# Strassen's seven block products for the first products of five pairs of F chunks in an exact-float32 MLP beside linear attention

## The chip, the cores and the metric

One of the cores of a Trainium2 chip runs the whole kernel. The metric is device time in microseconds (us), the median of several runs. The engines are called PE (TensorE, the matrix multiplier), DVE (VectorE), ACT (ScalarE), POOL (GpSimd) and SP (SyncE, which issues nearly all DMAs).

## The reference

A parallel block: one layernorm feeds linear attention with a learned feature map and an MLP, and both results are added to the input. B = 1, S = 2048 tokens, D = 640, H = 32 heads of 20, F = 1728; all arrays are float32.

```python
x  = A_x
xn = layernorm(x)
# attention
q, k, v = (xn @ wqkv) split into 3 x H heads of 20
pq, pk  = per head q @ w_phi, k @ w_phi
phi     = concat(softmax(p), softmax(-p))            # 40 features a head
o       = phi_q (phi_k^T v) / (phi_q (phi_k^T 1) + 1e-6)
A       = o @ wo
# MLP (its own layernorm: the block norms xn again)
y       = layernorm(xn)
B       = gelu(y @ w1 + b1) @ w2 + b2
return x + A + B
```

## The kernel before

**Arithmetic.** float32 is kept by splitting every operand into a high and a low part of the matmul type (`split`, L57-67: ACT copies to the high part, L61; another engine subtracts to get the low part, L64). A product is then three matmuls into one PSUM bank, `mm3` (L69-72): high·high (L70), high·low (L71), low·high (L72).

**Stages.** The tokens are four blocks of 512 (b0 to b3), D is five chunks of 128 (`KC`), F fourteen chunks of 128 (the last has 64). Activations lie transposed, features on partitions and tokens on columns.

1. First MLP pass (about 0 to 210 us): blocks b0 and b1. Beside it the generator `prep` makes what the next stage needs, one step per product: the folded q and k weights, and the normed tokens y of blocks b2 and b3 (L569-590: POOL subtracts the mean, DVE scales, ACT makes the high part, DVE the low part, two DMAs store both).
2. Projections and feature maps (about 210 to 441 us, `features`, matmuls at L673). For each token tile the features are transposed and stored to DRAM (`store_phi`).
3. Second MLP pass (441 to about 640 us): blocks b2 and b3, with attention's second half beside it.
4. Output projection (from about 640 us, L1119-1136), with sums into the accumulators and the stores.

**An MLP pass.** It works in groups g = 0 to 6 of two F chunks (a pair). `passes` (L267-309) does one group for one token block: for both chunks `first` (L256) makes z = w1·y as five `mm3` into one of banks 0 to 2; `gelu` (L263) applies the bias and gelu on ACT (L264) from the bank and splits the hidden block into high and low parts (ACT L61, DVE L64). The generator yields there; then for each of the five output chunks m two `mm3` (one for each F chunk) go into one of banks 5 to 7 and DVE adds the bank to the accumulator in SBUF (L309). The loop at L1081 starts the first products of the next group or block before it finishes the second products of the one before, so each gelu has the other block's second products to hide behind. Weights arrive by `fetch` (two DMAs of 320 KB, raw tiles r1 and r2) and are split by `take` (L229-254: ACT makes the high part, POOL the low part) a group ahead, into one of four slots w0 to w3 for each F chunk, w1 and w2 together.

**Attention beside the second pass.** `attend` (L1060) is a generator that `mm3`'s callers step once after each product (`next(self.beside, None)`). For each token block it loads 11 groups of features (tiles e); ACT makes the high part (L960), POOL the low part (L961), PE does two matmuls against kvs (L967, L968), ACT moves half of the result (L977), DVE adds (L978) into the output tile `ob`. `quotients` then moves denominators through DRAM, spreads their reciprocals with shuffles on DVE (L1011) and multiplies on POOL (L1013). Output tiles of b0 and b1 lie in a pool of their own (oB), those of b2 and b3 take over acc0 and acc1, which are free by then. `split` (L1017) divides them for the projection.

**What sets the order.** PE's order is written out by hand throughout. In the first pass and from pair 1 of the second pass on, DVE, ACT and POOL keep the written order too (`manual_schedule`); between them a scheduler orders these engines. SP's queue is ordered by a scheduler. Each engine works its list in order, and a tile that is taken again makes its new writer wait for its last reader.

The driver of the second pass, before:

```python
            this = mlp.passes(g, b, ws)
            next(this)
            for _ in before:
                pass
            before = this
...
            if g < 6:
                wn.append(mlp.take(2 * g + b))
                if 2 * g + b < 13:
                    mlp.fetch(2 * g + 1 + b)
```

Of the kernel before, what the change touches and what calls it, by code (L numbers as in the profile page):

```python
# [15 lines left out]
P = 128  # L16
# [35 lines left out]
def tile_kernel(ctx: ExitStack, tc: tile.TileContext, x, xT, wkT, wqT, wv, wphi, wo, w1, b1, w2, b2,  # L52
# [24 lines left out]
    ones1 = cp.tile([1, P], F32, name="ones1")  # L77
# [13 lines left out]
    r_dram = {n: tc.dram_tile([n, 8, P], F32, name=f"r{n}") for n in (1, 2)}  # L91
    a_dram = [tc.dram_tile([P, KC, 512], F32, name=f"a{b}") for b in range(2)]
# [108 lines left out]
    def load_rows(b):  # L201

        mr = mtile(5)
# [7 lines left out]
    class Mlp:  # L211
# [55 lines left out]
        def passes(self, g, b, ws, hid=None):  # L267
# [27 lines left out]
            for m in range(KC):  # L295
# [12 lines left out]
                else:  # L308
                    nc.vector.tensor_tensor(acc[b][:, m, :], pw, acc[b][:, m, :], op=ALU.add)  # L309

# [230 lines left out]
    def prep():  # L541
# [13 lines left out]
        mr = load_rows(2)  # L555
# [6 lines left out]


        def load(b, c):
            xc = fp.tile([P, D], F32, name="raw")[:, :512]
            nc.sync.dma_start(xc, xT[c * P:(c + 1) * P, b * 512:(b + 1) * 512])
            return xc

        for b in range(2, 4):  # L569
            ahead = load(b, 0)  # L570
            if b == 3:
                mr = load_rows(3)
            for _ in range(5 if b == 2 else 10):
                yield
            for c in range(KC):
                xc, ahead = ahead, load(b, c + 1) if c < KC - 1 else None
                nc.gpsimd.tensor_tensor(xc, xc, mr[:, 0], op=ALU.subtract)
                for _ in range(3):
                    yield
                nc.vector.tensor_tensor(xc, xc, mr[:, 1], op=ALU.mult)  # L580
                for _ in range(2):
                    yield
                hl = fp.tile([P, 2, KC, G5], F32R, name="t").rearrange("p a c f -> p a (c f)")[:, :, :512]
                nc.scalar.activation(hl[:, 0], xc, AF.Copy)
                for _ in range(2):
                    yield
                nc.vector.tensor_tensor(hl[:, 1], xc, f(hl[:, 0]), op=ALU.subtract)
                for p in range(2):
                    nc.sync.dma_start(y_dram[b - 2][p][:, c, :], f(hl[:, p]))
                yield  # L590
# [193 lines left out]
    for t, i in [(t, i) for t in range(14) for i in range(4)] + TAIL:  # L784
# [35 lines left out]
        if (t, i) == (11, 0):  # L820
            mlp = Mlp((0, 3, 2, 1), ((1, 2), (0, 3)))
            mlp.ph = ptile
            mlp.fetch(0)
        if (t, i) == (12, 3):
            with tc.issue_after(evac):
                ws = [mlp.take(0)]
            mlp.fetch(1)
        if (t, i) == (15, 3):
            w, late = mlp.take_parts(1)
            ws.append(w)  # L830
# [3 lines left out]
    mlp.fetch(2)  # L834
    wkv.close()

# [6 lines left out]
    kvs = bp.tile([P, 11, P], F32R, name="kvs")  # L843
    fs = ExitStack()
# [20 lines left out]
    load_acc(3)  # L865

# [50 lines left out]
    class Attention:  # L917

        def __init__(self, b, bank):
            self.b, self.n, self.bank = b, 0, bank  # L920
            self.ob = op.tile([P, KC, 512], F32, name=f"ob{b}") if b < 2 else acc01.tile([P, KC, 512], F32, name=f"acc{b - 2}")
# [61 lines left out]
        def quotients(self):  # L983
# [25 lines left out]
            for c in range(KC + 1):  # L1009
                if c < KC:  # L1010
                    nc.vector.stream_shuffle(rx[:, c, :], rx[:, c, :], SPREAD)  # L1011
                if c:
                    nc.gpsimd.tensor_tensor(ob[:, c - 1, :], ob[:, c - 1, :], rx[:, c - 1, :], op=ALU.mult)  # L1013
                for i in range(3):
                    yield

        def split(self, c, eng):  # L1017
# [15 lines left out]
            if c == KC and b < 2:  # L1033

                acc[b] = op.tile([P, KC, 512], F32, name=f"ob{b}")
                nc.sync.dma_start(acc[b], a_dram[b])

    def load_wo():

        for p, wd in enumerate(wo_dram):  # L1040
            w = wp.tile([P, 4, D], F32R, name=f"w{(2, 1)[p]}")
# [16 lines left out]
    ep = op = rx = None  # L1058
# [22 lines left out]
    for g in range(7):  # L1081
        for b in range(2, 4):
            if b == 2:
                wn = []
            if (g, b) == (0, 2):
                with tc.issue_after(subs["q", 15].ins):
                    wn.append(mlp.take(2))
                mlp.fetch(3)
# [111 lines left out]
```

## Time and profile before

| | |
|---|---|
| time, median of 3 runs | 720.99 us (720.93 to 721.01) |
| profiled execution, span | 719.3 us |
| profiled execution, time around the span (median less span) | 1.7 us |
| DMA traffic | 91.88 MB, mean 128 GB/s |
| HBM read, written | 63.51 MB, 27.73 MB |
| POOL, 441 to 470 us | 14.93 us busy |

The span runs from the first to the last instruction of one profiled execution. Rows of a time line give start, duration, engine, line and operation, output and inputs; rows of groups give the count, the busy time, the mean of one in ns, and the idle time of the engine just before them with what ended it. A matmul's row has the time from its start to its modelled end, and these overlap.

### The profile page before, as it was taken

The page shows a single profiled execution, that of the slowest core. Times are in us where ns is not written, and L with a number is a line of the kernel's source. Part 1 is how long each engine was busy: PE and PEld are TensorE (multiplying, and loading weights), DVE is VectorE, ACT ScalarE, POOL GpSimd, SP SyncE. Part 2 cuts the span into 40 slices and gives each one's busy share as a digit, 9 for nine tenths or more (in the row PEclk, how much of TensorE's full clock was granted, in tenths as well). Part 3 has the DMA queues.
Part 4 walks back from the last instruction along what each step waited for, and adds up shares of the span by engine and source line. Part 5 has one row for each costly group of instructions (what it writes and reads, how often), then busy time and mean ns, then how long its engine had stood idle before and what let it go on. Part 6 is the DMA issues. An engine that isn't in the chain of part 4 may idle for free.

```text
span 719.3 us, 9640 instructions
## 1 busy us (share of the span) xinstructions
PE 710.7 (99%) x3411; PEld 598.2 (83%) x3411; DVE 477.6 (66%) x787; ACT 323.0 (45%) x530; POOL 384.1 (53%) x332
## 2 busy tenths in 40 slices
PE   8989999999999999999999999999999999999998
PEld 7868888888888888888888887888888888888887
DVE  7776754757554788788898887635565566766432
ACT  6434454334334544545435446346565556530200
POOL 3521223345045997897878879346577787403000
PEclk9999999999999999999999999999999999999999
DMA  9803642656411227326302506943443443164122
GB/s 328 264 8 109 195 133 84 179 158 192 139 74 73 92 82 232 85 97 214 80 0 55 130 3 204 229 144 111 135 128 127 134 153 94 49 230 132 74 87 74
DMA packets 60454, 91.88 MB, mean 128 GB/s; under 512 B 7014, under 2 KB 31366, under 8 KB 59038
## 3 DMA queue, kind: packets, MB, share of 16 engines
q1 hardware_dynamic: 60102, 91.25, 40.7%
q8 instruction: 27, 0.44, 0.2%
q14 instruction: 21, 0.17, 0.1%
q10 hardware_dynamic: 304, 0.01, 0.0%
HBM read 63.51 MB, written 27.73 MB: 127 GB/s over the span
## 4 chain that ended last, share of the span: by engine, by line
PE 87%; DVE 3%; POOL 3%; ACT 1%; issue 1%; DMA 0%; SPq 0%; POOLq 0%
PE bank L673 23%; PE bank L70 18%; PE bank L72 18%; PE bank L71 18%; PE bank L743 2%; PE bank L499 2%; POOL m L708 2%; PE bank L967 1%; PE bank L968 1%; POOL m L719 1%; PE bank L305 1%; PE bank L285 1%; PE bank L304 1%; PE bank L286 1%; DVE sm L711 1%
## 5 line engine op out<-in xcount | busy, mean ns | idle before, releaser
L673 PE MATMUL bank<-wkh,y 128*128 128x512 f32 (+1 forms) x480 | 139.5, 364 | 0.0
L64 POOL TENSOR_TENSOR w<-r,w 128x640 fp32r<-128x640 f32 x52 | 83.3, 1619 | 95.6 <-ACT w L61 64.7
L70 PE MATMUL bank<-y,w 128*128 128x512 f32 (+1 forms) x334 | 129.8, 389 | 1.0 <-ACT m L264 1.0
L71 PE MATMUL bank<-y,w 128*128 128x512 f32 (+1 forms) x334 | 129.2, 387 | 0.0
L72 PE MATMUL bank<-y,w 128*128 128x512 f32 (+1 forms) x334 | 129.2, 387 | 0.0
L70 PE MATMUL bank<-m,w 128*128 128x512 f32 x260 | 102.4, 394 | 2.6 <-DVE acc L309 2.3
L72 PE MATMUL bank<-m,w 128*128 128x512 f32 x260 | 101.3, 389 | 0.0
L71 PE MATMUL bank<-m,w 128*128 128x512 f32 x260 | 101.2, 389 | 0.0
L673 PEld LDWEIGHTS bank<-wkh,y 128*128 128x128 f32 x480 | 87.5, 188 | 13.3
L309 DVE TENSOR_TENSOR acc<-bank,acc 128x512 f32<-128x512 f32 x120 | 81.1, 684 | 19.8 <-PE bank L72 11.8
L673 PE MATMUL bank<-wkl,y 128*128 128x512 f32 (+1 forms) x240 | 87.4, 364 | 0.0
L64 DVE TENSOR_TENSOR m<-m,m 128x512 fp32r<-128x512 f32 (+1 forms) x54 | 43.7, 814 | 65.5 <-ACT m L61 65.3
L70 PEld LDWEIGHTS bank<-y,w 128*128 128x128 f32 x334 | 62.7, 188 | 13.9 <-ACT m L264 1.2
L72 PEld LDWEIGHTS bank<-y,w 128*128 128x128 f32 x334 | 62.7, 188 | 12.8
L71 PEld LDWEIGHTS bank<-y,w 128*128 128x128 f32 x334 | 62.7, 188 | 12.5
L264 ACT ACTIVATE m<-bank,b1t 128x512 f32<-128x512 f32 (+1 forms) x54 | 36.2, 671 | 65.2 <-PE bank L72 61.0
L709 ACT ACTIVATE m<-m,rs_all 128x1280 f32<-128x1280 f32 x32 | 43.7, 1365 | 42.9 <-POOL m L708 42.9
L70 PEld LDWEIGHTS bank<-m,w 128*128 128x128 f32 x260 | 48.8, 188 | 14.4 <-DVE acc L309 3.5
L961 POOL TENSOR_TENSOR e<-e,m 128x512 fp32r<-128x512 f32 x28 | 36.2, 1295 | 41.8 <-ACT m L960 35.8
L711 DVE TENSOR_REDUCE sm<-m 128x64 f32<-128x1280 f32 x32 | 47.4, 1481 | 15.5 <-ACT m L709 15.4
L673 PE MATMUL bank<-w,y 128*128 128x512 f32 x240 | 57.4, 391 | 0.0
L72 PEld LDWEIGHTS bank<-m,w 128*128 128x128 f32 x260 | 48.8, 188 | 10.3
(156 smaller groups left out, 1249.3 us busy)
## 6 DMA issues: line engine op xcount, KB each, us to landing
r<-in_w SPq DMA_DIRECT2D x52, 320.0 KB
e<-e SPq DMA_DIRECT2D x40, 256.0 KB
e<-acc SPq DMA_DIRECT2D x52, 160.0 KB
acc<-in_xT SPq DMA_DIRECT2D x4, 1280.0 KB
xb<-in_x SPq DMA_DIRECT2D x8, 320.0 KB
t<-in_x SPq DMA_DIRECT2D x8, 320.0 KB
raw<-in_xT SPq DMA_DIRECT2D x10, 256.0 KB
yh<-t SPq DMA_DIRECT2D x10, 256.0 KB
```

The source lines that it names most:

```text
L64: eng.tensor_tensor(lo, src, f(hi), op=ALU.subtract)
L70: nc.tensor.matmul(ps, lh, rh, start=first, stop=False, **kw)
L71: nc.tensor.matmul(ps, lh, rl, start=False, stop=False, **kw)
L72: nc.tensor.matmul(ps, ll, rh, start=False, stop=last, **kw)
L264: nc.scalar.activation(gt, pz, AF.Gelu_apprx_tanh, bias=b1t[:, 2 * g + j:2 * g + j + 1])
L309: nc.vector.tensor_tensor(acc[b][:, m, :], pw, acc[b][:, m, :], op=ALU.add)
L499: nc.tensor.matmul(ps[:, u * nh * DF:(u + 1) * nh * DF], raw[:nh * DH, u * P:(u + 1) * P], wpt[:nh * DH, g, :nh, 1:], start=True, stop=True)
L673: nc.tensor.matmul(ps, lh[:, kc, c], rh[:, kc], start=n == 0, stop=n == 3 * KC - 1)
L708: subs[n, t] = nc.gpsimd.tensor_tensor(ep[:, s], a, b, op=ALU.subtract)
L709: exps[n, t] = nc.scalar.activation(e, e, AF.Exp, scale=rs_all[:, t:t + 1])
L711: nc.vector.tensor_reduce(sm, e.rearrange("p s (h f) -> p (s h) f", f=DH), axis=AX, op=ALU.add)
L961: nc.gpsimd.tensor_tensor(pl, e, f(ph), op=ALU.subtract)
```

## The change

For the pairs g = 1 to 5 of the second pass the first products of both token blocks are made together. With two F chunks (rows), two token blocks (columns) and two contraction chunks, z is a 2 x 2 block matrix that is the product of two 2 x 2 block matrices. The Winograd form of Strassen's method makes it from seven block products instead of eight:

- left: a11, a12, a22 (blocks of w1), s1 = a21 + a22, s2 = s1 - a11, s3 = a11 - a21, s4 = a12 - s2
- right: b11, b21, b22 (blocks of y), and t1 to t4, differences of y blocks: t1 takes the place of b12 less b11, and t2, t3, t4 are made of the same four blocks

Chunks 0 to 3 are done so (two products of 2 x 2 blocks, accumulated in the same banks), the fifth chunk plainly (`rest`). A bank goes on accumulating after ACT has copied it out (`copy`), so that shared partial sums are made once, and DVE adds banks to the copies (`add`). Gelu now reads SBUF.

What moves with it:

- The sums of w1 are made on POOL (four operations of 128x256 a pair, `sums`), their high part on ACT and low part on DVE (128x768, `split_sums`).
- Token differences are made in `prep`: eight subtractions on POOL, eight high parts on ACT, eight low parts on DVE, eight stores of 512 KB. Two loads of 1.5 MB bring t2 to t4 into new tiles tf0 and tf1; four of 256 KB put t1 over the chunks 0 and 2 of y of block b3; two of 512 KB put y back before pair 6.
- Weights are fetched and split by pair and by matrix (`fetch_pair`, `take_pair`): a slot has w1, or w2, of both chunks.
- The pool oB goes. Attention's outputs of b0 and b1 now also use acc0 and acc1, are stored (ten DMAs of 256 KB) and loaded again into tf0 and tf1 (two of 1.28 MB).

Instructions in the lists of the two programs, before and after: PE 3332 and 3302, ACT 535 and 568, DVE 769 and 802, POOL 337 and 365, SP 359 and 387.

```diff
+        def second(self, g, b, w, hid):
+            for m in range(KC):
+                pw = self.po()
+                ms = slice(m * P, (m + 1) * P)
+                for j, (hh, hl) in enumerate(hid):
+                    mm3(pw, w[:, 2 * j, ms], w[:, 2 * j + 1, ms], hh, hl, j == 0, j == 1)
+                    next(self.beside, None)
+                nc.vector.tensor_tensor(acc[b][:, m, :], pw, acc[b][:, m, :], op=ALU.add)
+                yield
...
+        def take_pair(self, g, second, slot):
+            w = wp.tile([P, 4, D], F32R, name=f"w{slot}")
+            def part(j, r):
+                hi, lo = w[:, 2 * j], w[:, 2 * j + 1]
+                if 2 * g + j < 13:
+                    split(hi, lo, r, eng=nc.gpsimd)
...
+        def sums(self, g):
+            raw = [r.rearrange("p (c f) -> p c f", f=P) for r in self.raw[g, False]]
+            (a11, a12), (a21, a22) = ((r[:, 0:4:2, :], r[:, 1:4:2, :]) for r in raw)
+            s = rp.tile([P, 3, 2, P], F32, name="s")
+            for out, x0, x1, op in ((s[:, 0], a21, a22, ALU.add), (a21, a11, a21, ALU.subtract),
+                                    (s[:, 1], s[:, 0], a11, ALU.subtract), (s[:, 2], a12, s[:, 1], ALU.subtract)):
+                nc.gpsimd.tensor_tensor(out, x0, x1, op=op)
+            self.raw[g, "s"] = s
+        def split_sums(self, g):
...
+            split(*hl, s)
...
+        def cross(self, g, bs, raw, sums, before, later):
...
+            def product(n, a, b, start=False):
+                for q in range(2):
+                    mm3(bank[n], left[a](0, q), left[a](1, q), right[b](0, q), right[b](1, q), start and q == 0, q == 1,
+                        skip_group_check=True)
+                    next(self.beside, None)
+            def rest(n, i, b):
+                mm3(bank[n], rows[i][0][:, 4], rows[i][1][:, 4], y[b][0][:, 4], y[b][1][:, 4], False, True, skip_group_check=True)
+                next(self.beside, None)
...
+            product("a", "a11", "b11", True)
+            copy(z11, "a")
+            product("c", "a12", "b21", True)
+            rest("c", 0, b0)
+            add(z11, "c")
+            gelu(z11, 0)
+            hi(z11, hid[0][0])
+            next(before)
+            lo(z11, hid[0][0])
+            product("b", "s1", "t1", True)
+            copy(z22, "b")
+            later[0]()
+            product("a", "s2", "t2")
+            copy(z12, "a")
+            next(before)
+            later[1]()
+            next(before)
+            product("a", "s3", "t3")
+            copy(z21, "a")
+            bank["c"] = banks.tile([P, 512], F32, name="bank2")
+            product("c", "a22", "t4", True)
+            rest("c", 1, b0)
+            add(z21, "c")
+            gelu(z21, 1)
+            hi(z21, hid[0][1])
+            product("b", "s4", "b22")
+            rest("b", 0, b1)
+            lo(z21, hid[0][1])
+            add(z12, "b")
+            gelu(z12, 0)
+            next(before)
+            rest("a", 1, b1)
+            add(z22, "a")
+            gelu(z22, 1)
+            for _ in before:
+                pass
...
+    for g in range(1, 6):
+        w2t, later = mlp.take_pair(g, True, 0 if g % 2 else 3)
+        hid, more = mlp.cross(g, (2, 3), raw, sums, before, later)
+        mlp.fetch_pair(g + 1, False)
+        for m, _ in enumerate(mlp.second(g, 2, w2t, hid[0])):
+            next(more, None)
+            if m == 0 and g < 5:
+                mlp.sums(g + 1)
+            if m == 1:
+                raw, parts = mlp.take_pair(g + 1, False, 1)
+                parts[0]()
+            if m == 2:
+                parts[1]()
+            if m == 3:
+                if g < 5:
+                    sums = mlp.split_sums(g + 1)
+                mlp.fetch_pair(g + 1, True)
+        before = mlp.second(g, 3, w2t, hid[1])
+    for p in range(2):
+        nc.sync.dma_start(f(y[3][p][:, 0:4:2]), y_dram[1][p][:, 0:4:2])
+    for b in range(2):
+        at[b].ob = tfp.tile([P, KC, 512], F32, name=f"tf{b}")
+        nc.sync.dma_start(at[b].ob, ob_dram[b])
```

Here `before` is the second product of block b3 of the pair before; each `next(before)` puts one output chunk of it (two `mm3`) between the new products. `later` are the two weight splits of w2, `more` the splits of the hidden blocks z12 and z22.

More of the change, by code (lines that the diff above doesn't have):

```diff
@@ L592, in load_v @@
+        tick = 0
+        for at, _, step, args in sorted(events, key=lambda e: e[:2]):
+            while tick < at:
+                tick += 1
+                yield
+            step(*args)
     def load_v():
@@ L1115, in tile_kernel @@
-    for _ in before:
-        pass
+    nothing = iter(())
+    mlp.beside = finish_kv(mlp.px)
+    with tc.issue_after(subs["q", 15].ins):
+        mlp.sums(1)
+    this = mlp.passes(0, 3, ws)
+    next(this)
+    finish(before)
+    before = this
+    for q in range(2):
+        for p in range(2):
+            nc.sync.dma_start(f(y[3][p][:, 2 * q]), t_dram[q][:, 0, p])
+    raw, parts = mlp.take_pair(1, False, 1)
+    for part in parts:
+        part()
+    sums = mlp.split_sums(1)
+    mlp.fetch_pair(1, True)
@@ L1119, in tile_kernel @@
+    finish(before)
     pw_ = Banks(6, 7)
```

221 lines of the change are left out of this document (147 added, 74 removed).

## The prediction

> **What bounds the kernel now.** I read four views in this order: the head of the page, the windows, the time line of PE, and PE's list of waits. The page first: shares of the span, granted clock, and the chain that ended last.
>
> ```profile
> span 719.3 us, 9640 instructions
> PE 710.7 (99%) x3411; PEld 598.2 (83%) x3411; DVE 477.6 (66%) x787; ACT 323.0 (45%) x530; POOL 384.1 (53%) x332
> PEclk9999999999999999999999999999999999999999
> PE 87%; DVE 3%; POOL 3%; ACT 1%; issue 1%; DMA 0%; SPq 0%; POOLq 0%
> ```
>
> TensorE is busy 99% of the span at full granted clock, and 87% of the last chain is its own work. The 719.3 us are one profiled execution; the median of the timed runs is 720.99, so 1.7 us lie around the span, and I add them at the end. The median's own spread (720.93 to 721.01) is small, so 0.2% (1.44 us) is about what a measurement of this kernel can tell from no change.
>
> A busy PE need not be a PE at its pace, so the windows come next (busy us per engine in order PE, PEld, DVE, ACT, POOL, then clock, DMA share, GB/s), and the spacing of its matmuls.
>
> ```profile
> 70.00:200.00 130.00, 130.00 (x609) 108.37 (x608) 81.09 (x142) 54.23 (x95) 42.36 (x28) 1.00 0.50 153
> 436.00:440.00 4.00, 4.00 (x19) 3.29 (x18) 2.46 (x3) 0.02 (x1) 4.00 (x5) 1.00 1.04 398
> 452.00:470.00 18.00, 18.00 (x110) 15.69 (x109) 9.73 (x17) 5.08 (x10) 5.34 (x3) 1.00 0.98 258
> 550.00:600.00 50.00, 50.00 (x222) 41.38 (x222) 31.05 (x50) 28.21 (x47) 36.08 (x27) 1.00 0.43 130
> ```
>
> ```profile
> 547.10 0.39 PE L70 MATMUL bank<-m,w 128*128 128x512 f32 x1
> ...
> 548.46 0.39 PE L70 MATMUL bank<-m,w 128*128 128x512 f32 x1
> ```
>
> Between those two starts lie six matmuls: 1.36/6 = 0.227 us each. The 0.39 us in the row is a duration that overlaps the next ones; the price of a 128x512 matmul is its spacing. The window agrees: 222 in 50 us is 0.225. The list of PE's waits (total us, times, longest) says that almost nothing stands between them:
>
> ```profile
> PE bank L70 <- DVE acc L309: 2.3, 2, 1.7
> PE bank L70 <- ACT m L264: 1.0, 1, 1.0
> ```
>
> So the second pass is a matmul count at a fixed spacing, and the other engines are hidden as long as they keep up.
>
> **What the change removes.** Each of the pairs 1 to 5 now takes 38 three-matmul products instead of 40. In the first product of a pair stand two F chunks and two token blocks, so four output blocks over five contraction chunks: 4 x 5 x 3 = 60 matmuls before, and 7 products x 2 chunk pairs x 3 + 4 x 3 (the fifth chunk, done plainly) = 54 after. Six fewer per pair, 30 in all; the second product stays at 60. The order of instructions of the two programs gives the same: 3332 instructions of PE to 3302, the difference all matmuls of 128x512. Saving: 30 x 0.227 = 6.8 us. It is on the path by itself, since PE is the bound, and is the ceiling of this change: 719.3 - 6.8 + 1.7 = 714.2.
>
> **What it adds.** Prices, from the groups of 490 to 640 us (x count, then busy, mean ns, idle before):
>
> ```profile
> L309 DVE TENSOR_TENSOR acc<-bank,acc 128x512 f32<-128x512 f32 x50 | 33.6, 682 | 4.5 <-PE bank L72 3.6 <-PE bank L305 0.3
> L961 POOL TENSOR_TENSOR e<-e,m 128x512 fp32r<-128x512 f32 x24 | 31.1, 1295 | 26.6 <-ACT m L960 21.9 <-PE bank L72 4.2 <-POOL e L961 0.5
> L64 POOL TENSOR_TENSOR w<-r,w 128x640 fp32r<-128x640 f32 x16 | 24.8, 1570 | 0.0
> L977 ACT ACTIVATE ts<-bank 64x512 f32<-64x512 f32 x37 | 21.9, 593 | 40.0 <-PE bank L968 37.8 <-DMA d<-ts 1.1 <-DMA o<-ts 1.1
> L1013 POOL TENSOR_TENSOR ob<-ob,rx 128x512 f32<-128x512 f32 x10 | 13.8, 1390 | 0.0
> L64 DVE TENSOR_TENSOR m<-m,m 128x512 fp32r<-128x512 f32 x18 | 13.7, 762 | 14.9 <-ACT m L61 14.8
> L264 ACT ACTIVATE m<-bank,b1t 128x512 f32<-128x512 f32 x18 | 12.4, 690 | 10.9 <-PE bank L72 10.2
> L61 ACT ACTIVATE w<-r 128x640 fp32r<-128x640 f32 x16 | 10.9, 728 | 0.8 <-PE bank L72 0.7
> L960 ACT ACTIVATE ph<-e 128x512 fp32r<-128x512 f32 x14 | 8.7, 620 | 0.1
> ```
>
> A round (one pair) has 114 matmuls and some 17 of the attention between them: 131 x 0.227 = 29.7 us. Into each go:
> - ACT: four bank copies at 0.6 (L977's row has half the partitions but the same 512 columns) and the high part of the weight sums, 128x768, 0.85 by 0.728 at 640 columns: 3.3 us. Window rate 28.21/50, or 16.8 per round: 20 of 29.7.
> - DVE: four adds from a bank at 0.68 and the low part of the sums, about 1.0: 3.7 us on 18.4, 22 of 29.7.
> - POOL: four sums of 128x256, a size that the trace does not show. Between 512 (1.295) and 640 columns (1.570) a column costs 2.15 ns, which leaves 0.19 us fixed; a row of another shape bears that out, 0.19 + 30 x 0.00215 = 0.26:
>
> ```profile
> L762 POOL TENSOR_TENSOR w<-sm,w 128x30 f32<-128x30 f32 x2 | 0.5, 254 | 0.0
> ```
>
> So one sum is about 0.75 and four are 3.0. The lower end is 0.65 (half of 1.295), the upper the 1.57 of a full weight tile, as the operands are read in strides. I take 0.75, as three rows stand on that line.
>
> POOL is the one to watch. The fullest round by the new order is the third: 9 subtractions of e at 1.295, 4 weight splits at 1.57, 4 sums at 0.75, 5 multiplications at 1.39: 11.7 + 6.3 + 3.0 + 7.0 = 28.0 of 29.7 us. The first two have no multiplications (21), the fourth has fewer subtractions, the fifth no sums.
>
> DVE and POOL also disturb each other:
>
> ```profile
> 529.58 0.69 DVE L64 TENSOR_TENSOR m<-m,m 128x512 fp32r<-128x512 f32 x1 [0.68 <-ACT m L61]
> ...
> 537.14 2.57 POOL L1013 TENSOR_TENSOR ob<-ob,rx 128x512 f32<-128x512 f32 x2
> ...
> 576.40 3.00 POOL L1013 TENSOR_TENSOR ob<-ob,rx 128x512 f32<-128x512 f32 x2
> ...
> 576.73 1.51 DVE L64 TENSOR_TENSOR m<-m,m 128x512 fp32r<-128x512 f32 x1 [0.70 <-ACT m L61]
> ```
>
> The low part of a hidden block takes 0.69 us with POOL idle and 1.51 when it meets POOL's pair of multiplications, which take 3.00 instead of 2.57: DVE loses 0.82, POOL 0.43. The mean over 18 is only 0.762, since nearly all now fall into gaps of POOL, gaps that the change fills. With five such DVE operations a round, POOL's third round is 28.0 + 5 x 0.43 = 30.2 of 29.7: full.
>
> The Trainium skill ("SBUF — State Buffer", section "Who interferes with whom") says just that: a VectorE instruction with two SBUF inputs and a GpSimd one that reads SBUF exclude each other for the whole instruction. The trace agrees, 0.69 against 1.51 us; the rule speaks against this change, which adds both kinds. Held against every meeting, it gives rival 1's time; with meetings only as often as their mean of 0.762 shows, the forecast's.
>
> **Where a new wait can reach PE.** Three places, by the new program order and the prices above.
> - The start of a round: PE's third matmul needs the low part of the pair's first weight tile, which POOL makes last. POOL comes there only behind the sums, and those stand behind a subtraction whose input ACT copies after the last gelu of the round. That gelu ends some 22 us into the round (its bank is done after about 90 matmuls, 20.4 us; then an add of 0.68 and 0.69 of gelu). Then 0.62 + 1.295 + 3.0 + 1.57 = 6.5: ready at 28.5, against 29.7 + 0.45 = 30.2. Slack 1.7; one or two meetings with DVE (0.43 each) leave about 1. Everything on PE is queued behind it.
> - s3·t3 goes into the bank that ACT has just copied after s2·t2: a copy of 0.6 behind whatever ACT is doing, against twelve matmuls of the second product that stand between (2.7 us): slack 1.3 to 2.1.
> - The accumulator's adds (L309) come later by the new DVE operations ahead of them; three banks in turn leave 1.1 to 2.4 us.
>
> I charge 1.2 us for all of it: between 0 (each slack holds) and 6 (POOL's fourth and fifth rounds start 2 late each, and the other three waits cost 2), nearest to the 1.0 to 2.3 us that PE's waits cost before with similar margins.
>
> **The rest, costed at nothing.** In the first pass 8 subtractions (1.3 on POOL), 8 high parts, 8 low parts and 8 stores of 512 KB are added beside 130 us in which POOL works 42, DVE 81, ACT 54 and the DMA engines are half used; without that cover it would be some 10 us of POOL. The preparation ends about 13 products (9 us) later; the weights of v are loaded behind it, with several us left. At the change of stage the DMA engines are full (0.98 from 452 to 470) while 4.2 MB of token combinations come in. At the 398 GB/s of 436 to 440 this takes 10.5 us, and PE comes to pair 1 at
>
> ```profile
> 462.32 0.39 PE L70 MATMUL bank<-y,w 128*128 128x512 f32 x1
> ```
>
> The first part of it that is needed late in the queue, t1 in y, I put 1 to 2 us before its use at about 467.8. Price between 0 and 3, taken as nothing, since POOL has two weight splits less there and stores begin earlier. Late in the pass 6.3 MB are added (attention outputs out and back, y back) to a DMA share of 0.43. With 10 products fewer before the last pair, attention ends at about the same time, and its last multiplication
>
> ```profile
> 656.67 2.54 POOL L1013 TENSOR_TENSOR acc<-acc,rx 128x512 f32<-128x512 f32 x2 [1.88 <-DVE rx L1011]
> ```
>
> is used 53 products (36 us) into the output projection, which would start near 633 instead of 640: some 10 us left.
>
> **Sum**: 719.3 - 6.8 + 1.2 = 713.7 in the profile, 715.4 measured.
>
> **Rivals.**
> 1. *POOL full in two rounds.* The exclusion above, plus time in which POOL waits for ACT (26.6 us before 24 subtractions in the row above, 1.1 each) that it can't make good. With 3 us a round not to be filled, round three needs 30.2 + 3 = 33.2 and is 3.5 late, the fourth some 2 late: 714.2 + 5.5 = 719.7, hardly a change. For it: 28 of 29.7. Against it: the waits for ACT overlap work that could go on ahead. Chance 0.16.
> 2. *The sums at the price of a full tile, which ends slower.* Place: the chain from the last gelu to the next round's first low part. At 1.57 each the four cost 6.3 instead of 3.0; the slack of about 1 leaves 2.3 late per round over four boundaries, and the same again in the full rounds three and four, where other work gives way: 4 x 2.3 + 2 x 1.2 = 11.6, or 714.2 + 11.6 = 725.8. It decides from 6.8/4 = 1.7 us late per boundary, that is sums of about 1.4. For it: strided operands. Against: the 128x30 row. Chance 0.14.
> 3. *Token combinations late at pair 1 and nothing else*: up to 3 us, 714.2 + 3 + 1.2 = 718.4. For it: a DMA share of 0.98. Chance 0.08.
> 4. *The products are not saved*: time unchanged or above by the added work, 721 to 723. The instruction order speaks against it. Chance 0.02.
>
> **How the numbers follow.** Forecast (714.2 plus 0 to 3 us) 0.60; rivals 0.16, 0.14, 0.08, 0.02. The predicted time is the forecast's own, 715.4. Low end 714.0 (no stall, a trifle of spacing); the high end takes in rivals 3 and most of 1: 720.2. Rival 2 and the edges, about 0.2, lie outside. Faster by over 0.2% (below 719.55): the forecast, rival 3 and half of rival 1: 0.76. Within: 0.07 of rival 1 and a little of 4: 0.08. Slower: rival 2 and what is left: 0.16.
>
> **What would show it.** Right: 30 matmuls fewer between 462 and 640, PE's spacing unchanged, its list of waits within 3 us of before, the output projection starting 5 to 7 us earlier; the sums near 0.75 in their own rows. Wrong: a wait of PE for POOL's weight tile at each start of a pair (rival 2, with sums near 1.5; rival 1, only at pairs 4 and 5), a wait for a load near 467 (rival 3), or spacing above 0.227 us in the new products, which no row of before can exclude.

## The result, and the profile after

The changed kernel takes 742.38 us (median of 4 runs, 741.77 to 744.8) against 721.0 before: 21.4 us slower, ratio 1.030 (95% interval 1.0287 to 1.0319). The forecast was 715.4. The head of its page, in the same order as before:

```profile
span 740.0 us, 9743 instructions
PE 715.0 (97%) x3381; PEld 593.6 (80%) x3381; DVE 515.6 (70%) x820; ACT 342.8 (46%) x563; POOL 422.4 (57%) x360
PEclk9999999999999999999999999999999989999999
PE 82%; DVE 7%; ACT 3%; POOL 1%; issue 1%; DMA 1%; DVEq 0%; ACTq 0%; POOLq 0%
```

PE has its 30 matmuls fewer (x3411 to x3381) and is nevertheless busy 4 us longer; the clock has an 8 in it; DVE and ACT have a share of the chain. PE's list of waits (total us, times, longest), whose largest entry before was 2.3 us:

```profile
PE bank L72 <- POOL w L64: 6.2, 2, 3.1
PE bank L70 <- DVE acc L322: 5.5, 5, 1.9
PE bank L1166 <- DVE acc L1177: 2.5, 2, 2.1
...
PE bank L1167 <- POOL e L1160: 1.1, 1, 1.1
```

L322 is the addition to the accumulator in the new second product, L1177 and L1160 attention's addition (L978 before) and subtraction (L961 before). The time line of PE shows three kinds of loss: a late start of pair 1, a stop at the start of pair 2, and slower products on the tiles tf.

```profile
463.92 0.40 PE L70 MATMUL bank<-y,w 128*128 128x512 f32 x1
...
492.87 0.40 PE L71 MATMUL bank<-y,w 128*128 128x512 f32 x1
496.39 0.80 PE L72 MATMUL bank<-y,w 128*128 128x512 f32 x1 [3.12 <-POOL w L64]
496.98 0.63 PE L70 MATMUL bank<-y,w 128*128 128x512 f32 x1
497.41 0.63 PE L71 MATMUL bank<-y,w 128*128 128x512 f32 x1
...
504.71 0.40 PE L70 MATMUL bank<-tf,w 128*128 128x512 f32 x1
...
506.11 0.39 PE L1166 MATMUL bank<-ph,kvs 128*128 128x512 f32 x1
```

Pair 1 starts 1.6 us later than before (463.92 against 462.32). Behind the gap of 3.5 us matmuls come 0.43 us apart, not 0.227. And six matmuls on tf take 1.40 us, 0.233 each. The same windows give the granted clock behind the two longest stops (columns as before):

```profile
497.00:500.00 3.00, 3.00 (x9) 2.38 (x8) 0.00 (x0) 0.60 (x1) 3.00 (x3) 0.54 0.68 170
601.00:605.00 4.00, 4.00 (x11) 3.13 (x10) 0.70 (x1) 1.71 (x3) 3.23 (x3) 0.50 0.67 200
```

From pair 1 on I took for every row the time to the next row less 0.227 us a matmul. Before, that leaves 0.2 us. After, it leaves 20.3 us in single stops, 3.4 in stretches at half pace (17 matmuls) and 2.2 in rows of 0.23 to 0.24 us. Less the 6.8 us saved that is 18.9; with 1.6 us ahead of pair 1 it makes 20.5 of the 20.7 us by which the spans differ. So the saving is there in full, and the costs (stops, half pace, spacing and the late start) are together four times as large.

### The profile page after: what moved, and what is told of

It reads as the page before. It is cut to its first block, busy times and chain, and to the rows that moved or that the text cites. A ratio compares the mean times of both kernels' runs of the same rounds, so it can differ in the third digit from the quotient of the medians.

```text
span 740.0 us, 9743 instructions
## 1 busy us (share of the span) xinstructions
PE 715.0 (97%) x3381; PEld 593.6 (80%) x3381; DVE 515.6 (70%) x820; ACT 342.8 (46%) x563; POOL 422.4 (57%) x360
## 4 chain that ended last, share of the span: by engine, by line
PE 82%; DVE 7%; ACT 3%; POOL 1%; issue 1%; DMA 1%; DVEq 0%; ACTq 0%; POOLq 0%
PE bank L860 27%; PE bank L70 16%; PE bank L72 15%; PE bank L71 15%; PE bank L930 2%; PE bank L658 2%; DVE acc L1177 1%; DVE rx L1210 1%; ACT ts L1176 1%; DVE m L421 1%; DVE m L412 1%; DVE acc L322 1%; PE bank L1167 1%; PE bank L1166 1%; DMA e<-e 1%
## 5 line engine op out<-in xcount | busy, mean ns | idle before, releaser
L64 POOL TENSOR_TENSOR w<-r,w 128x640 fp32r<-128x640 f32 x52 | 87.2, 1687 | 110.4 <-ACT w L61 79.6
L860 PE MATMUL bank<-wkh,y 128*128 128x512 f32 (+1 forms) x480 | 141.2, 368 | 0.0
L72 PE MATMUL bank<-y,w 128*128 128x512 f32 (+1 forms) x294 | 115.5, 393 | 6.2 <-POOL w L64 6.2
L70 PE MATMUL bank<-y,w 128*128 128x512 f32 (+1 forms) x294 | 115.8, 394 | 0.7 <-ACT m L266 0.7
L71 PE MATMUL bank<-y,w 128*128 128x512 f32 (+1 forms) x294 | 115.1, 392 | 0.0
L72 PEld LDWEIGHTS bank<-y,w 128*128 128x128 f32 x294 | 56.2, 191 | 18.8 <-POOL w L64 7.3
L70 PEld LDWEIGHTS bank<-m,w 128*128 128x128 f32 x260 | 48.9, 188 | 23.0 <-DVE acc L322 8.6
L70 PEld LDWEIGHTS bank<-y,w 128*128 128x128 f32 x294 | 56.1, 191 | 12.4 <-ACT m L266 0.9
L71 PEld LDWEIGHTS bank<-y,w 128*128 128x128 f32 x294 | 56.1, 191 | 11.4
L71 PEld LDWEIGHTS bank<-m,w 128*128 128x128 f32 x260 | 48.8, 188 | 10.6 <-DVE m L421 1.0
L72 PEld LDWEIGHTS bank<-m,w 128*128 128x128 f32 x260 | 48.8, 188 | 10.4
L311 DVE TENSOR_TENSOR acc<-bank,acc 128x512 f32<-128x512 f32 x70 | 47.1, 683 | 12.2 <-PE bank L307 6.4
L895 POOL TENSOR_TENSOR m<-m,mx 128x640 f32<-128x640 f32 (+2 forms) x48 | 44.4, 938 | 19.5 <-DVE mx L884 19.5
L1177 DVE TENSOR_TENSOR acc<-bank,ts 64x512 f32<-64x512 f32 x40 | 27.5, 687 | 39.8 <-ACT ts L1176 39.6
```

The source lines that it names most:

```text
L64: eng.tensor_tensor(lo, src, f(hi), op=ALU.subtract)
L70: nc.tensor.matmul(ps, lh, rh, start=first, stop=False, **kw)
L71: nc.tensor.matmul(ps, lh, rl, start=False, stop=False, **kw)
L72: nc.tensor.matmul(ps, ll, rh, start=False, stop=last, **kw)
L860: nc.tensor.matmul(ps, lh[:, kc, c], rh[:, kc], start=n == 0, stop=n == 3 * KC - 1)
L895: subs[n, t] = nc.gpsimd.tensor_tensor(ep[:, s], a, b, op=ALU.subtract)
```

## The experiments

Unless said otherwise each is a change to the changed kernel. "Order" below means which instruction stands ahead of which on one engine.

**First round: two orders, two start addresses.**

e1: the first weight split ahead of the sums.

```diff
-            if m == 0 and g < 5:
-                mlp.sums(g + 1)
-            if m == 1:
-                raw, parts = mlp.take_pair(g + 1, False, 1)
-                parts[0]()
+            if m == 0:
+                unsplit = mlp.raw[g + 1, False]
+                raw, parts = mlp.take_pair(g + 1, False, 1)
+                parts[0]()
+                mlp.raw[g + 1, False] = unsplit
+            if m == 1 and g < 5:
+                mlp.sums(g + 1)
```

> The changed kernel (742.4 us), with one reordering: the first weight split of the next pair (ACT high part, POOL low part) is put ahead of the four weight sums on POOL instead of behind them. Theory A (the order on POOL makes the first low part of a pair late): both waits of PE for POOL's weight tile (3.3 us each with what follows) go, and with them the stretches after them in which matmuls came at 0.425 instead of 0.227 us (3.4 us) and the 1.4 us wait for an e tile: 742.4 - 11.3 = about 731. Rival B (POOL is simply full, kept busy by its meetings with DVE): the lateness only moves to the sums, which the second product needs some 4.6 us into the pair; waits of 2 to 3 us appear there and the time stays at 739 to 743.

Measured 739.6 us (ratio to before 1.0263, 1.0248 to 1.0279). The waits for POOL's weight tile went, but those for attention's addition rose from 2.5 to 6.1 us and half pace did not go (4.0 us): nearer to B than to A.

e2: the accumulator's addition ahead of the attention step.

```diff
                     mm3(...)
+                    if j == 1:
+                        nc.vector.tensor_tensor(acc[b][:, m, :], pw, acc[b][:, m, :], op=ALU.add)
                     next(self.beside, None)
-                nc.vector.tensor_tensor(acc[b][:, m, :], pw, acc[b][:, m, :], op=ALU.add)
```

> The changed kernel, with one reordering on DVE alone: in the second products the addition of a bank to the accumulator is put ahead of the attention step that follows its last matmul, not behind it. Theory C (the accumulator's additions are late because they stand in DVE's queue behind an attention addition that waits for ACT): of the 7.0 us that PE waits for these additions some 5 go, 737 us. Rival (DVE is late because POOL locks it out, or because ACT is late): no change, 741 to 743.

Measured 739.7 us (1.0243 to 1.0285). The waits for L322 fell from 5.5 to 3.6 us and the time by 2.7, about half of the 5 us that were expected; the profiled execution is the slowest of the four (742.3 us).

e4 and e5: start addresses, `ones1` 36 instead of 4 bytes long in the changed kernel, 480 instead of 512 in the kernel before.

```diff
-    ones1 = cp.tile([1, 1], F32, name="ones1")
+    ones1 = cp.tile([1, 9], F32, name="ones1")
...
-    ones1 = cp.tile([1, P], F32, name="ones1")
+    ones1 = cp.tile([1, 120], F32, name="ones1")
```

> The changed kernel with all tiles on the left of SBUF moved up by 32 bytes (a constant is 36 bytes long instead of 4), so that they start at 32 above a multiple of 64, as in the kernel before and as the tiles on the right still do. Theory D (a matmul is 3% slower when one operand starts at a multiple of 64 bytes and the other at 32 above it): matmuls on the tf tiles go back from 0.233 to 0.227 us and those of the projection stage too, 1.7 + 2.0 us less: 738.7. Rival (it is the traffic, or the tile's place on the right): no change, 742.4.

> The kernel before, with all tiles on the left of SBUF moved down by 32 bytes, to multiples of 64; nothing else. Theory D (start addresses): the projection stage (210 to 441 us) gets about 1.7 us longer, its matmuls from 0.2300 to 0.2348 us on average, the second pass stays at 0.2267 since its weights and activations move together: 722.7. Rival (the slower spacing came from what the change does): 721.0.

e5 took 724.8 us against 720.9 (ratio 1.0052, 1.0037 to 1.0067): 32 bytes cost the kernel before 3.9 us, and nothing else had changed. That is 2.1 us more than theory D expected, for the second pass did not stay as it was: its products of y and m with w came 0.229 us apart on average, not 0.227. e4 gained nothing (743.9, 1.0304 to 1.0375; its four runs lie between 740.3 and 748.6 us, and its projection stage has 1159 matmuls in the window shown below), so theory D's rule of 64 bytes is wrong. That the tiles on the left had moved at all is the change's own doing: it shortens `ones1` from 512 to 4 bytes and sets a scratch area of 1 KB, which the list of what moves with it does not name. The projection stage shows the cost in its count of matmuls: 212 to 440 us, before, after, e5 (the change's times there are spacing alone, for PE is full in all three).

```profile
212.00:440.00 228.00, 228.00 (x1170) 196.96 (x1169) 183.43 (x266) 109.84 (x170) 185.45 (x184) 1.00 0.35 108
```

```profile
212.00:440.00 228.00, 228.00 (x1161) 195.23 (x1160) 183.38 (x266) 110.17 (x169) 183.40 (x181) 1.00 0.32 106
```

```profile
212.00:440.00 228.00, 228.00 (x1161) 195.12 (x1160) 183.42 (x266) 110.12 (x169) 183.48 (x181) 1.00 0.34 103
```

**Second round.** e6: all left tiles at 480 modulo 512, where they start in the kernel before and where nearly all right ones of these stages start in both, as the built programs place them.

```diff
-    ones1 = cp.tile([1, 1], F32, name="ones1")
+    ones1 = cp.tile([1, 121], F32, name="ones1")
...
-    nc = bacc.Bacc(..., dynamic_dma_scratch_size=1024)
+    nc = bacc.Bacc(..., dynamic_dma_scratch_size=512)
```

> The changed kernel with the tiles on the left of SBUF moved (a constant 480 bytes longer, a scratch area 512 bytes shorter) so that they start at 480 modulo 512, as all tiles on the left and most on the right do in the kernel before; in the changed kernel they start at 0, in the last two runs at 32 and 448, and both were slow. Theory D2 (full pace when the tiles on the left and on the right have the same start modulo 512): the projection stage is 1.6 us shorter, the tf products come at 0.227 instead of 0.233, all in all 3.6 us less, about 738.8. Rival (the pace hangs on something else in the layout): 742.

Measured 739.1 us (1.0237 to 1.0267), 0.3 from the expectation. Pair 1 starts at 462.57, and the tf products are back at 0.227 (six in 1.36 us); the projection stage has before's count:

```profile
212.00:440.00 228.00, 228.00 (x1170) 196.98 (x1169) 183.63 (x266) 109.92 (x169) 185.47 (x183) 1.00 0.36 110
```

```profile
504.19 0.39 PE L70 MATMUL bank<-tf,w 128*128 128x512 f32 x1
...
505.55 0.39 PE L1166 MATMUL bank<-ph,kvs 128*128 128x512 f32 x1
```

e7: DVE's low parts with one SBUF input.

```diff
-                nc.vector.tensor_tensor(h[:, 1], z, f(h[:, 0]), op=ALU.subtract)
+                nc.vector.tensor_tensor(h[:, 1], self.read, f(h[:, 0]), op=ALU.subtract)   # self.read: bank c
...
-            split(*hl, s)
+            nc.scalar.activation(hl[0], s, AF.Copy)
+            for o in (0, 384):
+                nc.vector.tensor_tensor(hl[1][:, o:o + 384], self.read[:, 0:384], f(hl[0][:, o:o + 384]), op=ALU.subtract)
```

> The changed kernel, but the low parts that DVE makes in pairs 1 to 5 (hidden blocks and weight sums) take their first input from a PSUM bank instead of SBUF, so that they have one SBUF input; the same count and size, and what they compute is not the product's low part. Theory L (DVE operations with two SBUF inputs and POOL's lock each other out): these operations take 0.7 (sums 1.2 in two) instead of up to 2.3 us, POOL's subtraction and split 1.3 and 1.57 instead of 2.1 and 2.3; the wait at the start of pairs 2 and 5 falls from 3.1 to about 1.5 us and the half-pace stretches behind it go: 742.4 - 3.2 - 3.4 - 2 = about 734. Theory A/C (order of the queues alone): the waits stay, 740 to 743.

Measured 731.1 us (1.0124 to 1.0154): 11.3 us less, with the order of the queues unchanged (the sums' low part is made in two steps, and that of pair 1 as before). L holds; orders alone would have left the time where it was. POOL gains too. Its weight splits from 464 to 640 us, the changed kernel and then e7:

```profile
L64 POOL TENSOR_TENSOR w<-r,w 128x640 fp32r<-128x640 f32 x19 | 32.9, 1735 | 8.9 <-ACT w L61 8.9
```

```profile
L64 POOL TENSOR_TENSOR w<-r,w 128x640 fp32r<-128x640 f32 x20 | 31.4, 1573 | 9.8 <-ACT w L61 9.8
```

In PE's list of waits those for POOL's weight tile fell from 6.2 to 1.4 us and those for attention's addition from 2.5 to 0.3, while those for the accumulator's additions stayed (5.5 in the changed kernel). The head of e7's list:

```profile
PE bank L70 <- DVE acc L322: 6.0, 5, 1.9
...
PE bank L72 <- POOL w L64: 1.4, 2, 1.1
```

e8: e1 and e2 together, and two gelus later on ACT; e9: the same at e6's addresses.

```diff
             add(z12, "b")
-            gelu(z12, 0)
             next(before)
+            gelu(z12, 0)
...
             add(z22, "a")
-            gelu(z22, 1)
             for _ in before:
                 pass
+            gelu(z22, 1)
```

> The changed kernel with three reorderings: the weight split ahead of the sums on POOL and the accumulator's additions ahead of the attention step on DVE (as in the first two runs, 739.6 and 739.7), and on ACT the last two gelus of a pair (z12, z22) placed one output chunk later, behind the attention copies of that chunk. Theory E (ACT's queue stands still at a gelu that waits for DVE's addition, which waits for PE; the attention copies behind it make DVE's additions late, and these PE): nearly all of the 20.3 us of waits and 3.4 us of half pace go, and the time is 722 to 726. Rival (DVE or POOL is simply full): 735 or more.

> The three reorderings of the run before and the tiles at 480 modulo 512. If theories D2 and E both hold the two gains add: 3.6 us less than that run, about 718 to 722. If D2 falls, the same as that run.

736.2 us (1.0199 to 1.0259) and 734.2 (1.0169 to 1.02). E is too strong: the order is worth 5 to 6 us, not 18. At the turn from pair 4 to pair 5 of e8 ACT now stands for POOL's sums, and DVE and PE behind it (ACT, DVE, PE):

```profile
592.49 0.74 ACT L61 ACTIVATE w<-r 128x640 fp32r<-128x640 f32 x1 [4.58 <-POOL r L366]
593.25 0.59 ACT L1177 ACTIVATE ts<-bank 64x512 f32<-64x512 f32 x1
...
593.87 0.69 DVE L1178 TENSOR_TENSOR acc<-bank,ts 64x512 f32<-64x512 f32 x1 [3.46 <-ACT ts L1177]
...
594.62 0.79 PE L1167 MATMUL bank<-ph,kvs 128*128 128x512 f32 x1 [3.25 <-DVE acc L1178]
```

**Third round: a version without most of the meetings.** e10 (at 480 modulo 512): z stays in PSUM, so that the low part has one input there, with nothing left out.

```diff
             def add(z, n):
-                nc.vector.tensor_tensor(z, bank[n], z, op=ALU.add)
+                nc.vector.tensor_tensor(bank[n], bank[n], z, op=ALU.add)
+                return bank[n]
...
-            add(z11, "c")
+            z11 = add(z11, "c")          # and so z21, z12, z22
...
-                for z, h in zip((z12, z22), hid[1]):
+                for z, h in zip((z22, z12), hid[1][::-1]):
```

> The changed kernel with the tiles at 480 modulo 512 (739.1 us), and z kept in its PSUM bank: DVE adds the copy to the bank in place, ACT makes gelu in place and the high part from it, and DVE makes the low part from bank and high part. Everything is computed as before; four of the five DVE operations with two SBUF inputs in a pair have one now (the weight sums' low part keeps two), and z22 is split ahead of z12. Theory L (lock between DVE and POOL): some 8 of the 11.3 us that the run without such operations gained, 731. Rival (banks held longer make PE wait for them): 738 or more.

Measured 730.8 us (1.0112 to 1.0159), 8.3 less than e6. DVE's groups from 464 to 640 us, the changed kernel and then e10:

```profile
L421 DVE TENSOR_TENSOR m<-m,m 128x512 fp32r<-128x512 f32 x20 | 22.1, 1104 | 2.6 <-ACT m L418 2.5
L64 DVE TENSOR_TENSOR w<-s,w 128x768 fp32r<-128x768 f32 x4 | 8.4, 2095 | 0.0
```

```profile
L422 DVE TENSOR_TENSOR m<-bank,m 128x512 fp32r<-128x512 f32 x20 | 13.6, 679 | 2.2 <-ACT m L419 2.1
L64 DVE TENSOR_TENSOR w<-s,w 128x768 fp32r<-128x768 f32 x4 | 4.9, 1234 | 0.0
```

The low part of a hidden block took 1.10 us on average beside POOL and 0.68 from PSUM; the sums' low part, still with two SBUF inputs, fell from 2.10 to 1.23.

e11 is e10 with e8's three orders; e12 also moves `split_sums` and then `parts[1]()` behind chunk 4, with the fetch of the next w2; e13 is e12 with attention's multiplications on `nc.vector`.

> The run before with the three reorderings of e8. If lock and order are two causes, the 4.9 us that these gave at 480 modulo 512 (739.1 to 734.2) come on top: 726. If both act through the same lateness of POOL, less: 728 to 731.

> The run before, with the second weight split of the next pair and the split of the sums moved from output chunks 2 and 3 to the end of chunk 4 of block 2's second products. In e8 the high part of this split made ACT wait 4.6 us for POOL's sums, and PE 3.3 us in turn for an attention addition, with half pace behind it. Theory F (ACT's queue blocked by a weight split that waits for POOL): 5 us less than the run before, 721. Rival (POOL full; the split becomes late for the products that need it): no gain.

> The run before with attention's 20 multiplications on DVE instead of POOL (0.69 instead of 1.3 us each). Theory B (POOL is full in the third and fourth pair, 28 of 29.7 us before any meeting): some 3 us less than the run before, 718. Theory L alone: each now meets POOL's subtractions as a DVE operation with two SBUF inputs, no gain or 1 to 2 us more.

724.1 us (1.0027 to 1.0057), 725.7 (1.0045 to 1.0078) and 733.2 (1.0143 to 1.0179). Order and lock are two causes: the order is worth 6.7 us once most of the meetings are gone (e10 to e11), and 4.9 with them (e6 to e9). F fails, for the stop changes its place (3.3 us of PE for attention's subtraction on POOL). In e13 each multiplication on DVE has two SBUF inputs; the 15 that fall before 640 us take 0.89 us on average instead of 0.69, and PE's single stops rise from 7.7 in e12 to 14.8 us. How much of that is meetings and how much is DVE's added work was not separated. In e11's time line from pair 1 on 6.6 us of stops and 2.4 of half pace are left, most of it one event three matmuls into pair 5. There, as in e8, ACT has stood for POOL's sums at the turn of the pairs (4.1 us):

```profile
584.48 0.39 PE L72 MATMUL bank<-y,w 128*128 128x512 f32 x1
587.79 0.80 PE L1168 MATMUL bank<-ph,kvs 128*128 128x512 f32 x1 [2.93 <-DVE acc L1179]
588.40 0.80 PE L1169 MATMUL bank<-e,kvs 128*128 128x512 f32 x1
```

**Last rounds: the stop behind pair 4.** The expectations call it the stop in pair 4, where the work that causes it stands. All runs are changes to e11. e14: `nc.vector` for two of five multiplications of blocks 0 and 1 (`self.b < 2 and c in (2, 4)`); e15: for block 1's five; e16: `nc.vector` for the sums of pairs 2 to 5 (its expectation counts them as 3 to 6; those of pair 1 stay on POOL). Each edit replaces `nc.gpsimd` in one line.

> e11 (724.1 us) with two of the five multiplications of token blocks 0 and 1 on DVE instead of POOL. Theory B (POOL's backlog in pair 4 makes the sums late, ACT waits for them, and PE for ACT): POOL gets 2 x 1.3 us shorter there, the stop of 3.1 us and the half pace behind it (6.2 us in all) go or shrink below 1 us: 718 to 720. Theory L alone (moved to DVE the multiplications lock as they did with all 20 moved): 724 to 727.

> e11 with all five multiplications of token block 1 on DVE; those are the ones that fall into pair 4. Theory B: the stop in pair 4 goes, 718 to 719, unless the five DVE operations with two SBUF inputs cost 1 to 3 us by their meetings: 719 to 722. Theory L alone: 724 or more.

> e11 with the weight sums of pairs 3 to 6 (four operations of 128x256 for each pair that has them) on DVE instead of POOL. Theory B: POOL is 3 us shorter in each of these pairs and the stop goes: 718 to 720. Theory L: four more short operations with two SBUF inputs, each waiting up to 1.3 us for POOL, make DVE's additions late instead: 724 to 728.

724.7, 725.0 and 723.9 us (intervals 1.0036 to 1.0066, 1.004 to 1.008, 1.003 to 1.0063): no gain that can be told. The stop itself does follow POOL's backlog, as theory B says: it shrinks to 2.1 us in e14 and to 0.7 in e15, which moves the multiplications that stand there. But in e15 these five take 1.10 us each on DVE, and six other stops of 0.6 to 1.4 us come, where e11 had one. In e16 the stop grows to 4.6 us. Two of e16's four sums of one pair on DVE, the first unhindered, the last beside POOL:

```profile
580.40 0.41 DVE L366 TENSOR_TENSOR s<-r 128x256 f32<-128x256 f32 x1
...
583.69 1.64 DVE L366 TENSOR_TENSOR s<-r,s 128x256 f32<-128x256 f32 x1
```

e17: sums in the middle of the pair; e18: block 1's multiplications later; e19: both.

```diff
             hi(z21, hid[0][1])
+            mid()                        # mlp.sums(g + 1) for g < 5
             product("b", "s4", "b22")
...
             later[1]()
+            self.fetch_pair(g + 1, False)
             next(before)
...
-            for i in range(6):
+            for i in range(24 if self.b == 1 else 6):
                 yield
             for c in range(KC + 1):
```

> e11 (724.1 us) with the weight sums of the next pair made on POOL in the middle of the pair (behind the high part of z21, where POOL stands idle for some 4 us waiting for ACT) instead of its end; their raw tiles are fetched as soon as the second split of w2 has freed them. Theory G (coincidence: sums, splits, multiplications and subtractions fall into the same 18 us of POOL, and PE waits for what stands last): the stop of 3.1 us with its half pace goes, 718. Rival (the raw tiles land too late and POOL, standing in order, waits for them): 724 or more, with a wait of POOL for a load in each pair.

> e11 with the multiplications of token block 1 some 18 products (12 us) later, so that they fall behind the sums of pair 5. Theory G: the stop goes, 718 to 720. Rival (the multiplications only meet the next pair's splits): 722 to 725.

> Both moves. Theory G: not more than the better of the two, 717 to 719, since one stop can go only once; it would be faster than the kernel before (721.0) by 2 to 4 us.

723.8 (1.0029 to 1.0057), 732.3 (1.0152 to 1.018) and 732.6 us (1.015 to 1.0178). In e17 the stop behind pair 4 shrank to 0.5 us and one of 2.8 us came in pair 3, where sums and a multiplication now stand ahead of the subtraction that PE needs (POOL):

```profile
540.78 0.73 POOL L366 TENSOR_TENSOR s<-r 128x256 f32<-128x256 f32 x1
...
543.80 1.26 POOL L1216 TENSOR_TENSOR acc<-acc,rx 128x512 f32<-128x512 f32 x1
545.02 1.26 POOL L1164 TENSOR_TENSOR e<-e,ph 128x512 fp32r<-128x512 f32 x1
```

The rival's wait for raw tiles is there too (7.4 us of POOL's idle time in four places), but PE's list names none. In e18 and e19 DVE stood still, which stopped PE for 13 and 10 us (e18, then e19):

```profile
613.21 0.68 DVE L1179 TENSOR_TENSOR acc<-bank,ts 64x512 f32<-64x512 f32 x1 [17.72 <-DMA rx<-d]
```

```profile
613.09 0.68 DVE L1181 TENSOR_TENSOR acc<-bank,ts 64x512 f32<-64x512 f32 x1 [15.75 <-DMA ob<-acc]
```

These are attention's first addition into the output tile of block 3, which is the tile of block 1's output. The late multiplications made the stores of that output late (the last is issued at 603.3 us in e18), and the addition has to wait for them. The first row names a load of `rx`, which this addition does not use; the second names the store.

The best versions, e11, e16 and e17, are 3 us slower than the kernel before. None beats it.

## Why the prediction was wrong

**Right.** 30 matmuls at 0.227 us: they are gone, and the 6.8 us stand in the account. The sums: 0.74 us where they meet no DVE operation and 0.87 on average, 0.75 predicted, so rival 2 named the right place with a wrong price. POOL's fullest pair is the third, with 29.6 us of work (28.0 predicted, 30.2 with meetings), yet no wait for its weight tile follows it. PE waits for no load at pair 1 (rival 3), the first pass hides its part (in e6 pair 1 starts only 0.25 us later than before), and no entry of PE's list names a late DMA.

**The step that failed: "I charge 1.2 us for all of it".** It measured 20.3 us of stops and 3.4 of half pace. Three parts of it were wrong.

*The chain at the start of a round.* POOL and DVE of the changed kernel around the end of pair 1:

```profile
487.24 1.30 POOL L1160 TENSOR_TENSOR e<-e,ph 128x512 fp32r<-128x512 f32 x1 [4.06 <-ACT ph L1159]
488.49 0.74 POOL L365 TENSOR_TENSOR s<-r 128x256 f32<-128x256 f32 x1
...
491.98 2.14 POOL L1160 TENSOR_TENSOR e<-e,m 128x512 fp32r<-128x512 f32 x1
494.08 3.75 POOL L64 TENSOR_TENSOR w<-r,w 128x640 fp32r<-128x640 f32 x2
...
492.94 2.00 DVE L64 TENSOR_TENSOR w<-s,w 128x768 fp32r<-128x768 f32 x1
```

Its order was as said as far as the sums, but between them and the split stands a second subtraction that my sum left out (1.3 us), and this one met the sums' low part: 2.14 instead of 1.3 on POOL, 2.00 instead of about 1.0 on DVE. The gelu ended 22.7 us into the pair instead of 22, and PE reached the next pair after 28.7 us instead of 29.7. Against a slack put at 1.7 us the split came 3.1 us late. The same wait stands at the start of pair 5, but not at those of pairs 3 and 4.

*The meetings.* I had seen both sides (DVE loses 0.82, POOL 0.43) and charged POOL's 0.43 alone; the mean of 0.762 that I took for their frequency came from a schedule whose gaps the change filled, as the text itself said, and it became 1.10. By e7 the meetings cost 11.3 us, by e10, which keeps one of the five, 8.3. They reach PE mostly through POOL's weight tile and attention's addition, whose waits e7 nearly removes; the waits for the accumulator's additions owe them little, for e7 leaves these at 6.0 us. This is the exclusion that rival 1 builds on (chance 0.16, 719.7 us), but not at its place: it named the starts of pairs 4 and 5, and PE's two waits for the weight tile stand at pairs 2 and 5. The Trainium skill ("SBUF — State Buffer", section "Who interferes with whom") says that a VectorE instruction with two SBUF inputs contends with GpSimd's reads, and one with at most one does not. Here 1.10 us with two and 0.68 with one agree with it.

*The queue behind a wait.* I listed the waits at PE, not what stands behind each on ACT and DVE. The changed kernel at the end of pair 4, ACT, DVE, PE:

```profile
586.64 0.72 ACT L415 ACTIVATE m<-m,b1t 128x512 f32<-128x512 f32 x1 [0.59 <-DVE m L412]
587.39 0.59 ACT L1176 ACTIVATE ts<-bank 64x512 f32<-64x512 f32 x1
...
588.01 0.70 DVE L1177 TENSOR_TENSOR acc<-bank,ts 64x512 f32<-64x512 f32 x1 [1.41 <-ACT ts L1176]
588.74 0.69 DVE L322 TENSOR_TENSOR acc<-bank,acc 128x512 f32<-128x512 f32 x1
...
589.49 0.51 PE L70 MATMUL bank<-m,w 128*128 128x512 f32 x1 [1.94 <-DVE acc L322]
```

The gelu now waits for a DVE addition (before: for PE's bank alone); attention's copy stands behind it on ACT, its addition on DVE, the accumulator's addition behind that, and PE needs the bank. The order on the queues is what removes these waits for the accumulator's additions (0.6 us in e11, against 4.1 in e10), and with most of the meetings and the addresses out of the way it is worth 6.7 us (e10 to e11).

**The step that was missing: spacing.** "PE's spacing unchanged" was what I expected to see, with tf's left open. By e6 the start addresses cost 3.3 us, by e5 a shift of 32 bytes does 3.9 us to the kernel before, and no term of the sum has them.

**What stays open.** e11 is 10 us above 714.2: its stops (6.6), half pace (2.4), spacing (0.4) and a start of pair 1 that is 0.8 later account for it. Each way of removing its one large stop brought another. Whether an order exists without any is not shown, and fewer pairs in this form were not tried. By the count of matmuls a version with none of these losses would take about 714 us, 1% less than the kernel before.

## What to carry to other kernels

Where PE is full, the work that replaces matmuls goes to engines that wait on each other: trace for each new operation the queue that stands behind it, not its duration alone. When POOL's gaps are filled, price every DVE operation with two SBUF inputs at its met duration (here 1.1 to 2.1 us, not 0.7 to 1.0), or give it an input in PSUM. And when tiles move in memory, compare the spacing of untouched matmuls first, since that shift alone was 3 to 4 us here.

## What the runs showed of the hardware

*Start addresses.* With left and right tiles at the same start modulo 512 (before, e6) 1170 matmuls of the projection stage ran in 228 us, and 1159 to 1161 with the left ones at 0, 32 or 448 and the right ones at 480 (the changed kernel, e4, e5); the tf products came at 0.227 us in e6 and at 0.233 in the changed kernel. Why is not shown, nor that 512 is the step that counts. That in e5 and in the changed kernel products with both operands on the left were slower too (0.229 us on average in the second pass) is not explained by this rule.

*Half pace after a stop.* Behind a stop of 3.3 us, and behind two of 3.2 and 1.4 us close together, the clock was granted at about 0.5 for 3 to 5 us, which cost 1.2 and 2.2 us more. Single stops of 2.1 and 2.3 us in the same trace had no such effect, but in e1 stops of 2.1, 2.3 and 2.6 us did. The Trainium skill ("TensorE: Matmul & The Clock Gate", Part 1) describes a gate that halves the clock after an idle window of about 3.4 us, free-running, and gives 426.7 ns for a cold matmul of 512 columns; the 0.43 us here agree, while the stops of e1 are shorter than that window. Its warm figure, 215.7 ns, is below the 227 of these traces. In both the measurement decides. A window that runs on its own could also be why executions of the changed kernel differ by 3 us (741.77 to 744.8) and those of the kernel before by 0.1; that is argued, not shown.
